# Loads of q, k and v that each wait for the fifth load ahead of them

## The chip, the cores and the metric

The kernel runs on one core of one Trainium2 chip. The metric is the device time of one execution in microseconds (us), the median over several runs. A core has five engines that run side by side, each with its own stream of instructions: TensorE (PE in the profile; its weight loads are shown apart as PEld), VectorE (DVE), ScalarE (ACT), GpSimd (POOL) and SyncE (SP). SyncE does no arithmetic here: it waits on semaphores and issues transfers (DMAs), and sixteen DMA engines move the bytes. SP issues strictly in order, so a transfer that has to wait holds up all that stands behind it on SP.

## The reference: linear attention, then a mixture of experts

For each of 8 batches and 8 heads (576 positions, 64 channels) the reference makes a 64x64 state from k and v, multiplies q by it and normalises each row. The rows of all heads, side by side, are 4608 tokens of 512 channels. A token whose skip score is positive goes to the one of 8 experts with the highest gate value, and gets that expert's output added.

```
kv  = einsum('bhsd,bhse->bhde', k, v)
o   = einsum('bhsd,bhde->bhse', q, kv)
x   = o / sqrt(mean(o*o) + 1e-6) * g_norm          # -> (4608, 512)
go  = x @ w_skip > 0
e   = argmax(x @ w_gate);  p = softmax(x @ w_gate)[e]
out = x + (go ? p * (relu(x @ w1[e]) @ w2[e]) : 0)
```

## The kernel before

**Two stages.** The first 110 us or so are attention; the rest is the experts, whose work is matrix products on PE with the experts' weights (8 x 4 MB) streamed in beside them. The change lies in the first stage.

**Loads.** For each batch b, k, v and q are each loaded as four parts (`load_part`, L116); part j holds the head pair 2j and 2j+1 for all 576 positions: 128 partitions by 9 x 64 float32, 288 KB. A batch is thus 12 loads, the whole stage 96. `load_kv` (L129) issues k part 0, v part 0, k part 1 and so on; `load_q` (L138) issues the four parts of q. All go out on SP. k and v have three buffers each, q has two, so a load of batch b+3 (or b+2 for q) also waits until PE has done with the batch that held its buffer. In program order the loads run: k and v of batch 0, q of batch 0, k and v of batch 1, q of batch 1, k and v of batch 2, then one group at a time from the loop over units (L1001 to L1005), with stores of finished rows (`store_x`, L652) between them on the same SP queue.

**Semaphores of the loads.** The framework gives each DMA of SP or ACT one of eight semaphores in turn, and a DMA waits until the one that had its semaphore before, the eighth ahead, has landed. The four small DMAs that ACT issues at the start take four of these turns. So at most eight are under way.

**Work on PE in the first stage.** `state(b, some)` (L379) is a run of small 64x64 products k^T v, accumulated in `sum_ps`; it reads parts 0 and 1 in its first half and parts 2 and 3 in its second. `state_t` and `state_m` (L406, L414) transpose the state and multiply it by the gate weights. The 36 *units* n each take half the heads (u = 0 or 1) of four of the nine 64-row chunks of one batch, or of the ninth chunks of four batches: `turn(n)` (L460) transposes q for the next unit, `values(n)` (L495) multiplies by the state; a unit with u = 0 reads q parts 0 and 1, one with u = 1 parts 2 and 3. ACT squares and copies, DVE sums, normalises and scales (`xl`, L554), POOL multiplies by g_norm (`xb`, L628). The order of all of this is written out by hand (`tc.manual_schedule()`): `at(step, part, job)` puts a job at a step of the loop over units, and each engine does its instructions in that order.

**Instructions themselves** are also brought in by DMA: the profile shows them as the kind "instruction", on queues of their own (q8 and q14).

Of the kernel before, what the change touches and what calls it, by code (L numbers as in the profile page):

```python
# [17 lines left out]
def kernel(  # L18
# [43 lines left out]
    nc = tc.nc  # L62
# [48 lines left out]
    g_ps = ps_g.tile([P, 512], FP32)  # L111
    GB = 4 * KD + 8 * G

    kts, vts, qts = {}, {}, {}

    def load_part(t, src, b, j):  # L116

        js = slice(j, j + 1)
        nc.sync.dma_start(
            out=t[:, js, :, :].rearrange("p j c d -> p j (c d)"),  # L120
            in_=src[b].rearrange("(j a) (p c) d -> (a p) j (c d)", a=2, c=C)[:, js, :])

    def load(pool, tag, src, b):
        t = pool.tile([P, 4, C, D], FP32, tag=tag, name=tag)
        for j in range(4):
            load_part(t, src, b, j)
        return t

    def load_kv(b, js=range(4)):  # L129
        if b < B:  # L130
            if js.start == 0:
                for name, to in (("k", kts), ("v", vts)):
                    to[b] = kv_pool.tile([P, 4, C, D], FP32, tag=name, name=name)
            for j in js:
                for src, t in ((k, kts[b]), (v, vts[b])):
                    load_part(t, src, b, j)
# [201 lines left out]
    def load_weights(r, pool, behind=None, later=False):  # L338
# [4 lines left out]
        if behind:  # L343
            tc.add_manual_dep(ins.ins, behind.ins.name, WAIT, reason="gathers first")
        w2 = pool.tile([P, FC, DM], FP32, tag="w2", name="w2")
# [4 lines left out]
    def load_second(r, behind=None):  # L350
# [3 lines left out]
        if behind:  # L354
            tc.add_manual_dep(ins.ins, behind.ins.name, WAIT, reason="gathers first")

# [89 lines left out]

    late = []
    todo = {}
    WAIT = mybir.DependencyInfo(mybir.DependencyClass.Sync, mybir.DependencyReason.SCHED_ONLY)

    def at(step, part, job):
        todo.setdefault((step, part), []).append(job)
# [188 lines left out]
    def scale(n, behind=None, keep=0, eng=None):  # L641

        while len(late) > keep:
            job, nq, store = late.pop(0)
            ins = job(eng or nc.gpsimd)
            if behind:
                tc.add_manual_dep(ins.ins, behind.ins.name, WAIT, reason="VectorE's port is free then")
            store = store() if store else None
# [1006 lines left out]
```

## Time and profile before

| | |
|---|---|
| median of 3 runs | 369.1 us (367.73 to 369.5) |
| the profiled execution, its own time | 368.61 us |
| its span, first to last instruction | 366.7 us |
| PE busy | 349.8 us (95%) |
| bytes moved by DMA | 81.70 MB |
| mean granted clock of TensorE | 0.997 |

The profile is of one execution. "Busy tenths in 40 slices" cuts the span into 40 pieces of 9.17 us and gives the share of each in which an engine (or, on average, the 16 DMA engines) was at work. A wait is written as the waiting engine and line, an arrow, and what ended the wait; "issue" there means that nothing that the profile shows was being waited for. "To landing" is the time from the issue of a DMA to its completion. In a timeline row stand the start, the length, the engine and line, the operation with its output and inputs, how many instructions are merged in the row, and in brackets the idle time of the engine before it.

### The profile page before, as it was taken

Reading aid. Unit: us, or ns where it says so; the run is one execution under the profiler, and the core shown is the slowest. Engines: PE = TensorE matmul, PEld = TensorE weight load, DVE = VectorE, ACT = ScalarE, POOL = GpSimd, SP = SyncE. Lnnn points to the kernel's source line nnn. Section 1 sums busy time; section 2 is a strip of 40 time slices with the busy share of each in tenths; the row PEclk is TensorE's granted clock in tenths of the full one; section 3 lists DMA queues with packets and bytes.
Section 4 is the critical chain, followed back from the end, with each engine's and each line's share of the span. In section 5 each row is a group of like instructions: output and inputs, shape, how many; then the busy total and the mean of one; then the engine's idle time right before and its main releaser. Section 6 shows DMA issues by size and latency. Waiting matters only on the chain.

```text
span 366.7 us, 9560 instructions
## 1 busy us (share of the span) xinstructions
PE 349.8 (95%) x3754; PEld 304.6 (83%) x3754; DVE 247.6 (68%) x630; ACT 147.0 (40%) x424; POOL 123.2 (34%) x201
## 2 busy tenths in 40 slices
PE   8979998999899998999999999999999999999993
PEld 4768887889779667599879988989988998989982
DVE  2646678678889553875937676686776776878821
ACT  2537675677855323345104402511431430531410
POOL 8037677757784170223032102303203203002002
PEclk9999999999999999999999999999999999999998
DMA  7999999999969479782526437365563662601001
GB/s 258 378 389 389 391 384 389 394 351 305 348 214 362 121 255 374 285 261 77 220 85 231 145 142 240 126 231 155 193 230 102 231 247 73 221 1 57 3 2 53
DMA packets 32808, 81.70 MB, mean 223 GB/s; under 512 B 3242, under 2 KB 3250, under 8 KB 32756
## 3 DMA queue, kind: packets, MB, share of 16 engines
q1 hardware_dynamic: 29264, 70.53, 54.2%
q0 software_dynamic: 3472, 10.48, 8.8%
q8 instruction: 31, 0.51, 0.5%
q14 instruction: 21, 0.17, 0.1%
q10 hardware_dynamic: 20, 0.02, 0.0%
HBM read 66.80 MB, written 14.48 MB: 222 GB/s over the span
## 4 chain that ended last, share of the span: by engine, by line
PE 79%; issue 7%; DMA 4%; DVE 3%; POOL 2%; ACT 2%; SPq 0%; POOLq 0%; DVEq 0%; ACTq 0%
PE bank L1279 45%; PE bank L1211 9%; PE o_ps L507 6%; DMA v<-in_v_dram 4%; PE sum_ps L387 4%; PE bank L1199 4%; PE q_ps L469 3%; PE bank L1180 2%; DVE xl L554 1%; DVE rs L531 1%; PE o_ps L488 1%; PE q_ps L876 1%; PE g_ps L876 1%; POOL xb L628 1%; PE g_ps L417 1%
## 5 line engine op out<-in xcount | busy, mean ns | idle before, releaser
L1289 ACT COPY p<-bank 128x128 f32<-128x128 f32 (+6 forms) x70 | 20.8, 297 | 96.8 <-PE bank L1279 89.3
L1279 PE MATMUL bank<-xt,w 128*128 128x128 f32 (+5 forms) x336 | 55.4, 288 | 0.4 <-DVE bank L1283 0.4
L1410 POOL DMA_INDIRECT out_dram<-xg,rows x14 | 14.0, 997 | 116.5 <-DVE xg L1407 114.2
L1279 PEld LDWEIGHTS bank<-xt,w 128*128 128x128 f32 x336 | 47.0, 190 | 2.3 <-DVE bank L1283 1.8
L1283 DVE TENSOR_TENSOR bank<-bank,p 128x128 f32<-128x128 f32 (+6 forms) x70 | 23.6, 337 | 30.0 <-PE bank L1279 27.6
L628 POOL TENSOR_TENSOR xb<-xl,g_b 128x512 f32<-128x512 f32 x26 | 31.7, 1221 | 15.0 <-DVE rs L545 12.1
L1279 PE MATMUL bank<-xs,s 128*128 128x128 f32 (+5 forms) x224 | 36.7, 289 | 0.0
L507 PE MATMUL o_ps<-kvd,qT 128*128 128x146 f32 x240 | 35.4, 289 | 0.7 <-DVE xl L554 0.5
L507 PEld LDWEIGHTS o_ps<-kvd,qT 128*128 128x128 f32 x240 | 31.4, 189 | 1.9 <-DVE xl L554 1.3
L1279 PEld LDWEIGHTS bank<-xs,s 128*128 128x128 f32 x224 | 31.1, 190 | 1.0 <-issue 0.5
L1211 PE MATMUL bank<-w,ht 128*32 128x128 f32 (+2 forms) x424 | 29.9, 313 | 0.0
L387 PE MATMUL sum_ps<-v,k 64*64 64x64 f32 x1152 | 24.5, 223 | 4.7 <-issue 4.3
L531 DVE TENSOR_REDUCE rs<-sq 128x8 f32<-128x512 f32 x36 | 24.5, 681 | 5.2 <-ACT sq L523 5.0
L387 PEld LDWEIGHTS sum_ps<-v,k 64*64 64x64 f32 x1152 | 20.2, 134 | 9.2 <-issue 6.1
L554 DVE TENSOR_TENSOR xl<-o_ps,rs 128x584 f32<-128x584 f32 x32 | 24.5, 766 | 3.9
L1211 PEld LDWEIGHTS bank<-w,ht 128*32 128x32 f32 (+2 forms) x424 | 18.2, 119 | 10.6 <-issue 7.2
L1279 PE MATMUL bank<-t,ht 128*128 128x256 f32 x112 | 27.0, 384 | 0.0
L1279 PE MATMUL bank<-w,ht 128*128 128x256 f32 x112 | 26.5, 380 | 0.0
L1171 POOL DMA_INDIRECT xg<-out_dram,src x14 | 13.9, 992 | 35.2 <-DMA out_dram<-xg,rows 19.0
L1279 PE MATMUL bank<-t,hs 128*128 128x256 f32 x112 | 25.3, 379 | 0.0
L523 ACT ACTIVATE sq<-o_ps 128x512 f32<-128x512 f32 x34 | 20.2, 595 | 11.3 <-PE o_ps L507 10.5
L1279 PEld LDWEIGHTS bank<-t,ht 128*128 128x128 f32 x112 | 20.8, 190 | 3.9 <-issue 1.2
(217 smaller groups left out, 671.9 us busy)
## 6 DMA issues: line engine op xcount, KB each, us to landing
w<-in_moe_w_dram SPq DMA_DIRECT2D x16, 2048.0 KB, 10.1
k<-in_k_dram SPq DMA_DIRECT2D x32, 288.0 KB, 6.0
v<-in_v_dram SPq DMA_DIRECT2D x32, 288.0 KB, 6.2
q<-in_q_dram SPq DMA_DIRECT2D x32, 288.0 KB, 6.0
out_dram<-xb SPq DMA_DIRECT2D x25, 256.0 KB, 5.9
out_dram<-w SPq DMA_DIRECT2D x8, 256.0 KB, 5.5
out_dram<-xb POOLq DMA_DIRECT2D x3, 256.0 KB
xg<-out_dram,src POOLq DMA_INDIRECT x16
```

Source lines behind the costliest of these rows:

```text
L387: nc.tensor.matmul(out=sum_ps[w * 64:(w + 1) * 64, a, u, :], lhsT=kt[r, 2 * u + w, c, :], rhs=vt[r, 2 * u + w, c, :], start=(c == 0), stop ...
L507: mm = nc.tensor.matmul(out=ps[:, w, 0:2 * PK].rearrange("p (r k) -> p r k", r=2)[:, :, cols], lhsT=qT[:, w, a, :], rhs=kvds[b % KVD][:, w ...
L523: nc.scalar.activation(out=sq[:, :, :, :], in_=heads(ps, G, G + 2 * D), func=ACT.Square)
L531: nc.vector.tensor_reduce(out=rs[:, :, :], in_=sq[:, :, :, :].rearrange("p x y (a d) -> p x (y a) d", a=2), axis=AX.X, op=ALU.add)
L554: nc.vector.tensor_tensor(out=xl[:, :, :, :].rearrange("p x y (a k) -> p x (y a) k", a=2), in0=ps[:, :, 0:2 * PK].rearrange("p x (h k) -> ...
L628: late.append((lambda eng: eng.tensor_tensor(out=xb[:, :, 4 * u * D:(4 * u + 4) * D].rearrange("p r (w x) -> p r w x", w=2), in0=xl[:, :, ...
L1199: nc.tensor.matmul(out=hps[:, cols], lhsT=w_sb[r][0][:, dc, f * P:(f + 1) * P], rhs=xt[:, dc, cols], start=(dc == 0), stop=(dc == DC - 1))
L1211: nc.tensor.matmul(out=yps[q * m:(q + 1) * m, 0:n], lhsT=ht(f)[:, off:off + m], rhs=w_sb[r][1][:, f, q * n:(q + 1) * n], start=(f == 0), s ...
L1279: nc.tensor.matmul(out=out, lhsT=lhsT(i), rhs=rhs(i), start=start and i == 0, stop=i == k - 1, skip_group_check=True)
L1283: nc.vector.tensor_tensor(out=to, in0=x, in1=y, op=ALU.add)
L1289: nc.scalar.copy(out=t, in_=x)
L1410: ins = nc.gpsimd.indirect_dma_start(out=cut_rows(m)[:, :], out_offset=bass.IndirectOffsetOnAxis(ap=rows[:, col:col + 1], axis=0), in_=x, ...
```

## The change

Each load of q, k or v, from the thirteenth in program order on, gets one more dependency: on the load five places ahead of it in the list of these loads. Stores are not in that list. The first twelve loads (k, v and q of batch 0) are left as they were. The line that makes `WAIT` only moves up. Nothing else changes: no other engine's instructions, no sizes, no order.

```diff
-    kts, vts, qts = {}, {}, {}
+    kts, vts, qts, loads = {}, {}, {}, []
+    PACED, DEPTH = 12, 5
+    WAIT = mybir.DependencyInfo(mybir.DependencyClass.Sync, mybir.DependencyReason.SCHED_ONLY)
 
     def load_part(t, src, b, j):
 
         js = slice(j, j + 1)
-        nc.sync.dma_start(
+        ins = nc.sync.dma_start(
             out=t[:, js, :, :].rearrange("p j c d -> p j (c d)"),
             in_=src[b].rearrange("(j a) (p c) d -> (a p) j (c d)", a=2, c=C)[:, js, :])
+        if len(loads) >= PACED:
+            tc.add_manual_dep(ins.ins, loads[-DEPTH].ins.name, WAIT, reason="a short queue")
+        loads.append(ins)
...
-    WAIT = mybir.DependencyInfo(mybir.DependencyClass.Sync, mybir.DependencyReason.SCHED_ONLY)
```

What SP waits for, on SP's stream from the twelfth load on. In these rows `DMAHW0` to `DMAHW7` are the eight semaphores of SP's and ACT's DMAs, and the loads take them in turn (the first load of the kernel has `DMAHW4`). Before:

```order
L119 DMA q_110<-in_q_dram 128x576 [waits DMAHW7_49]
L119 DMA k_269<-in_k_dram 128x576 [waits DMAHW0_49]
L119 DMA v_270<-in_v_dram 128x576 [waits DMAHW1_49]
L119 DMA k_269<-in_k_dram 128x576 [waits DMAHW2_49]
L119 DMA v_270<-in_v_dram 128x576 [waits DMAHW3_49]
L119 DMA k_269<-in_k_dram 128x576 [waits DMAHW4_49]
L119 DMA v_270<-in_v_dram 128x576 [waits DMAHW5_49]
```

and with the change:

```order
L121 DMA q_110<-in_q_dram 128x576 [waits DMAHW7_49]
L121 DMA k_269<-in_k_dram 128x576 [waits DMAHW3_49,DMAHW0_49]
L121 DMA v_270<-in_v_dram 128x576 [waits DMAHW4_49,DMAHW1_49]
L121 DMA k_269<-in_k_dram 128x576 [waits DMAHW5_49,DMAHW2_49]
L121 DMA v_270<-in_v_dram 128x576 [waits DMAHW6_49]
L121 DMA k_269<-in_k_dram 128x576 [waits DMAHW7_49]
L121 DMA v_270<-in_v_dram 128x576 [waits DMAHW0_49]
```

The thirteenth load (the first of k of batch 1) waited for the eighth DMA ahead of it, and now waits for the fifth load ahead too; from the sixteenth on the nearer wait stands alone, since it implies the farther one.

Later on SP, around the load of q of batch 3 (`q_759`), where two stores stand between the loads. Before:

```order
L119 DMA k_595<-in_k_dram 128x576 [waits DMAHW2_49]
L119 DMA v_596<-in_v_dram 128x576 [waits DMAHW3_49]
L670 DMA out_0_dram<-xb_485 64x1024 [waits DMAHW4_49,Pool_49]
L670 DMA out_0_dram<-xb_485 64x1024 [waits DMAHW5_49]
L119 DMA q_759<-in_q_dram 128x576 [waits DMAHW6_49,PE_49]
L119 DMA q_759<-in_q_dram 128x576 [waits DMAHW7_49]
L119 DMA q_759<-in_q_dram 128x576 [waits DMAHW0_49]
L119 DMA q_759<-in_q_dram 128x576 [waits DMAHW1_49]
```

and with the change:

```order
L121 DMA k_595<-in_k_dram 128x576 [waits DMAHW5_49]
L121 DMA v_596<-in_v_dram 128x576 [waits DMAHW6_49]
L674 DMA out_0_dram<-xb_485 64x1024 [waits Pool_49]
L674 DMA out_0_dram<-xb_485 64x1024
L121 DMA q_759<-in_q_dram 128x576 [waits DMAHW7_49,PE_49]
L121 DMA q_759<-in_q_dram 128x576 [waits DMAHW0_49]
L121 DMA q_759<-in_q_dram 128x576 [waits DMAHW1_49]
L121 DMA q_759<-in_q_dram 128x576 [waits DMAHW2_49]
```

The k and v loads wait three places nearer; the stores wait for POOL alone (what they waited for before has already been waited for by the load ahead of them); and the q loads wait only one place nearer than before, since the two stores between are not counted.

## The prediction, made before the changed kernel was run

> **What bounds the kernel now.** First the head of the page, then the slices of DMA use.
>
> ```profile
> span 366.7 us, 9560 instructions
> PE 349.8 (95%) x3754; PEld 304.6 (83%) x3754; DVE 247.6 (68%) x630; ACT 147.0 (40%) x424; POOL 123.2 (34%) x201
> DMA  7999999999969479782526437365563662601001
> GB/s 258 378 389 389 391 384 389 394 351 305 348 214 362 121 255 374 285 261 77 220 85 231 145 142 240 126 231 155 193 230 102 231 247 73 221 1 57 3 2 53
> q8 instruction: 31, 0.51, 0.5%
> k<-in_k_dram SPq DMA_DIRECT2D x32, 288.0 KB, 6.0
> ```
>
> PE is the engine that is nearly always at work, and the end of the kernel is PE's. But in the first eight slices (to 73 us) the DMA engines are full as well, at 378 to 394 GB/s. A load of 288 KB (294,912 bytes) at 392 GB/s takes 0.75 us, and 6.0 us from issue to landing is eight times that: the loads stand in a line of eight and come out one each 0.75 us. So in that stretch a load lands when the line has moved on, not when it was issued.
>
> Next, who waits: PE and POOL in the first 110 us, SP to 75 us.
>
> ```profile
> PE sum_ps L387 <- issue: 4.3, 3, 2.4
> PE sum_ps L387 <- DMA v<-in_v_dram: 0.3, 1, 0.3
> ...
> POOL xb L628 <- DVE rs L545: 12.1, 17, 2.1
> ...
> SPq L119 <- DMA k<-in_k_dram: 9.2, 22, 0.9
> SPq L119 <- PE g_ps L409: 1.1, 1, 1.1
> ```
>
> PE waits for a load once, for 0.3 us. Its longest idle is three stalls, 4.3 us in all, in the middle of `state`, and nothing the profile names ends them. SP waits mostly for loads and little for PE's buffers, so the loads set their own pace. PE's timeline has the stalls, and one more row that matters:
>
> ```profile
> 24.47 0.62 PE L387 MATMUL sum_ps<-v,k 64*64 64x64 f32 x25 [2.43 <-issue]
> 45.69 0.66 PE L469 MATMUL q_ps<-ident,q 128*128 128x128 f32 x4
> 63.38 0.57 PE L387 MATMUL sum_ps<-v,k 64*64 64x64 f32 x21 [0.99 <-issue]
> 69.87 0.56 PE L387 MATMUL sum_ps<-v,k 64*64 64x64 f32 x19 [0.84 <-issue]
> ```
>
> What are the stalls? From one to the next I count instructions, and ask which instruction transfers run in the 1.2 us before each ends (the windows 22.0 to 23.2, 60.7 to 61.9, 67.3 to 68.5):
>
> ```profile
> 24.40:63.30 38.90, 37.17 (x755) 32.77 (x755) 27.43 (x61) 27.07 (x73) 27.85 (x55) 1.00 1.05 388
> 63.30:69.80 6.50, 5.64 (x126) 5.08 (x127) 5.29 (x13) 3.27 (x8) 5.13 (x8) 1.00 1.05 392
> ...
> q8 instruction: 1, 0.02, 5.6%
> ...
> q8 instruction: 1, 0.02, 5.7%
> ...
> q8 instruction: 1, 0.02, 5.6%
> ```
>
> The first two counts are PE's products and weight loads: 1510 and 253 instructions, that is six times 252 and once 253. The q8 queue brings 31 blocks of 16 KB for 7508 such instructions, 242 each. Each window holds one block, and the stall ends 1.3 to 1.5 us after its window closes. So PE has come to the end of a block and the next one has not arrived: the stalls are late instruction fetches. One thing is missing: no row shows when a fetch is asked for. If it is asked for when PE begins the block before (251 instructions earlier, about 57.6 us for the second stall and 63.4 for the third), the block starts to move 3.1 and 3.9 us after that.
>
> **The change, part by part.** *Loads under way: 8 to 5.* Nothing is removed, and no instruction is added on PE, DVE, ACT or POOL. On SP a load is issued three landings later, 3 x 0.75 = 2.25 us. Does it land later? With five under way the line gives each load 5 x 0.75 = 3.75 us from issue to landing. A load that meets no line needs this long (the k loads issued in the first 2 us, and, as the far bound, the rate at 4.9 to 11.5 us, when five to eight loads were under way):
>
> ```profile
> DMA to landing us min/median/max: 3.5/4.0/4.5
> ...
> 4.90:11.50 6.60, 6.46 (x138) 3.91 (x140) 2.59 (x28) 0.72 (x3) 3.29 (x6) 1.00 0.98 335
> 12.00:45.60 33.60, 30.80 (x607) 27.21 (x601) 19.08 (x43) 21.34 (x57) 17.13 (x33) 1.00 1.05 392
> ```
>
> 3.5 is under 3.75, by 0.25 us only: the line still just closes, and loads land when they landed before. Bounds of what this costs: nothing, or the rate falls from 392 to 335 GB/s. At that rate the 42 loads from the thirteenth to the fifty-fourth take 0.88 instead of 0.75 us each, 5.4 us more. I take 1% of the 33.6 us, 0.3 us, an estimate near the lower bound, because the full-rate row covers five times the stretch and the early row also has loads at its start that wait for ACT's small ones.
>
> *Does a later load hold PE up?* The row of PE at 45.69 is the first turn of q of batch 3, which reads parts 0 and 1. Part 3 was issued and landed so:
>
> ```profile
> 41.93 0.43 SPq L119 DMA_DIRECT2D q<-in_q_dram  x1
> ...
> DMA to landing us min/median/max: 5.2/5.2/5.2
> ```
>
> 41.93 + 5.2 = 47.1, and two landings earlier part 1 came, at 45.6. PE used it at 45.69: a margin under 0.1 us. So up to here PE cannot run ahead of the loads, whatever stalls it is spared; and every us by which loads fall behind by then is lost to PE at once. Hence the 2.43 us stall at 22.05 is worth nothing if it goes: PE would only wait at 45.6 for q instead. That is the next thing late.
>
> *The two later stalls.* After 45.69 the loads are further ahead. The tighter ones are those of q, with two buffers where k and v have three. For batch 4: issue of the parts, their time to landing, and the first turn on PE; for the last part of batch 7, issue and landing, and the turn that reads it:
>
> ```profile
> 51.89 2.12 SPq L119 DMA_DIRECT2D q<-in_q_dram  x4
> DMA to landing us min/median/max: 6.3/6.3/6.3
> 60.88 0.63 PE L469 MATMUL q_ps<-ident,q 128*128 128x128 f32 x4
> ...
> 87.93 0.43 SPq L119 DMA_DIRECT2D q<-in_q_dram  x1
> DMA to landing us min/median/max: 5.4/5.4/5.4
> 96.78 0.66 PE L469 MATMUL q_ps<-ident,q 128*128 128x128 f32 x4
> ```
>
> The four parts of batch 4 are all issued by 54.0 and landed by 60.3; part 3 of batch 7 lands at 93.3 and is used at 96.78. Here a stall that goes is PE's gain. If a fetch block stands in the same line as the loads, its wait shrinks with the line: three loads fewer are 2.25 us less. The stalls need only 0.99 and 0.84 us (1.13 and 0.98 on the weight loads), so both go even if the block feels half of that. Is the gain on the chain? The chain from 58 to 75 us:
>
> ```profile
> 62.39 0.99 issue
> 63.38 0.57 PE sum_ps L387 x21
> ...
> 68.34 1.18 POOL xb L628
> 69.52 1.36 issue
> ```
>
> The second stall is on it. At 69.52 the chain moves to POOL; POOL's own row there,
>
> ```profile
> 70.90 0.85 POOL L400 COPY kvd<-both 64x256 f32<-64x256 f32 x2 [1.39 <-ACT both L394]
> ```
>
> waits for the copy of the state, which waits for the products that the third stall holds up. So both count: 0.99 + 0.84 = 1.8 us. All engines after that follow PE, and the margin of 3.5 us at q of batch 7 is more than what they gain, so 1.8 us passes to the end.
>
> *Queued behind the waiting loads on SP* are the stores L670. They go out about 2 us later, but still into a full DMA line. Who waits for them is POOL, for an `xb` buffer; POOL's waits before L628 are for DVE in the row above (12.1 us, 17 times), so the six buffers cover it: nothing, and up to 2.25 us a store if that cover were gone. The double waits of a few loads cost SP an instruction or so beside an issue of 0.33 us each 0.75 us: nothing.
>
> *The sum.* -1.8 us (two stalls) + 0 (first stall, absorbed at q of batch 3) + 0.3 (rate) = -1.5 us. The profiled execution took 368.61 us, so 367.1; it stood 0.5 us under the median of 369.1, so I put the median at **367.6 us**.
>
> **The rivals.** *The fetch does not stand in the loads' line.* If each DMA engine takes packets in turn from its queues, a fetch waits for one packet of 2 KB, not for the loads ahead, and a shorter line changes nothing: the stalls stay, and with 0.3 us for the rate the time is 369.4 us. For it: block delays after the assumed request differ much while the line is always full. Against it: in the full stretch the block moves 3 to 4 us after the request, far more than one packet of about 0.1 us. The Trainium skill, "DMA: Bandwidth & Descriptors", section "Queues, rings and completion order", says just this of the engines: they go round between the queue rows, one packet from each. By that rule the two stalls keep their 1.8 us; the 3.1 and 3.9 us above speak against it, though they rest on an assumed time of request.
>
> *The line no longer closes, slower.* The price is at q of batch 3, 45.6 us, the first place without margin. If a load needs more than 3.75 us from semaphore to landing, each load after the twelfth comes later by a fifth of the excess, 42 times. At 4.1 us this is 0.07 x 42 = 2.9 us; less 1.8 for the stalls, +1.1; from 4.2 us on it is slower by over 0.5%. At the early rate (5.4 us) it would be +3.6, 372.7 us. For it: only 0.25 us of margin, and the 16 engines do not finish a load together, so a short line starves the quick ones. Against: landings are regular to a few hundredths of a us at 392 GB/s.
>
> *Fetches everywhere gain.* ACT, DVE and POOL fetch instructions too, and PE's idle of 0.5 to 0.8 us on DVE and ACT at 58, 95 and 99 us might shrink a little: -1.8 and another 1 us, 366.3 us. Little speaks for it; those waits have named causes.
>
> **How the numbers follow.** Forecast (both stalls go, the rate about holds): 0.42. Fetch unchanged: 0.20. Slower rate: 0.24. More gained: 0.14. No change is what this kernel's measurement cannot tell from 369.1, within 0.5% or 1.85 us. The forecast at -1.5 lies close to that edge: I count a third of it, 0.14, as faster. Faster 0.14 + 0.14 = 0.28; slower 0.24; same 0.48. Range: from 366.0 (more gained, with the spread of the three runs) to 371.2 (a rate loss of some 4 us less the stalls); outside are the larger rate losses and a rest below, about 0.2. The forecast's own range is 366.6 to 368.4.
>
> **What would show it.** Right: k, v and q land a median of 3.7 to 4 us after issue; the slices to 73 us keep 385 GB/s or more; the rows of PE at 62 and 69 us have no idle; q of batch 3 is turned at 45.6 to 46 us, with a wait for q before it if the first stall went. Wrong: landing still 5 to 6 us; slices at 370 or less, and PE waiting for q, k or v by more than 1 us; stalls of the old size with the shorter line. What would break the sum is chiefly the margin of 0.25 us.

## The result and the profile after

The changed kernel takes **379.1 us** (median of 6 runs, 375.69 to 380.97) against 369.05 us beside it (6 runs, 367.73 to 370.72): a ratio of **1.025**, 95% interval 1.0215 to 1.029. It is slower by 10 us. The prediction, 367.6 us with a range to 371.2, was wrong, and in sign. Medians and ratios leave out runs over 1.5% above the fastest of their kernel: four of the ten with six loads under way (376.2 us and more), three of the ten with seven (372.1 us and more), the profiled ones among them, and two of the nineteen beside those.

The profiled execution took 378.42 us. The head, the slices, two shares of the chain and two DMA groups of its page:

```profile
span 376.5 us, 9562 instructions
PE 354.7 (94%) x3754; PEld 308.1 (82%) x3754; DVE 248.5 (66%) x630; ACT 146.9 (39%) x424; POOL 123.8 (33%) x201
PEclk9999899998799999999999999999999999999998
DMA  7989999999999849955626363672762662700001
GB/s 270 338 296 364 328 323 315 337 314 326 346 329 282 298 124 339 390 196 214 205 80 216 118 225 85 221 265 60 248 223 81 246 219 95 251 1 34 24 1 53
PE 67%; DMA 22%; issue 6%; DVE 3%; POOL 1%; SPq 0%; ACT 0%; POOLq 0%; DVEq 0%
k<-in_k_dram SPq DMA_DIRECT2D x32, 288.0 KB, 5.0
q<-in_q_dram SPq DMA_DIRECT2D x32, 288.0 KB, 5.3
```

From 9 to 75 us the DMA tenths still read 9, but for one slice of 8, while the rate has gone from 378 to 394 GB/s down to 296 to 364: the engines count as busy and move less. A load lands 5.0 to 5.3 us after its issue (median), where I had expected 3.7 to 4. The chain that ended last has 22% of DMA in place of 4%. The chain before was

```profile
PE 79%; issue 7%; DMA 4%; DVE 3%; POOL 2%; ACT 2%; SPq 0%; POOLq 0%; DVEq 0%; ACTq 0%
```

In the PEclk row of the changed kernel three slices (38 to 47, 85 to 94 and 94 to 104 us) have fallen to 8, 8 and 7 tenths.

The changed kernel by windows, with the columns as in the prediction (the last three are granted clock, DMA share and GB/s):

```profile
12.00:45.60 33.60, 27.80 (x496) 24.53 (x495) 15.90 (x37) 17.44 (x48) 13.97 (x27) 0.95 0.96 324
39.90:43.40 3.50, 3.50 (x45) 3.31 (x44) 1.66 (x3) 1.88 (x8) 1.40 (x2) 0.51 0.97 321
91.20:98.00 6.80, 5.91 (x52) 5.06 (x53) 2.42 (x7) 1.95 (x4) 1.39 (x2) 0.50 0.99 371
```

In the stretch that ran at 392 GB/s before, the rate of all transfers is now 324: 294,912 bytes each 0.91 us instead of 0.75. Twice TensorE runs at half clock, for 3.4 and 6.8 us. Who waits on PE up to 112 us:

```profile
PE q_ps L473 <- DMA q<-in_q_dram: 7.1, 7, 2.3
PE sum_ps L392 <- issue: 1.6, 2, 1.0
PE sum_ps L392 <- DMA v<-in_v_dram: 1.4, 2, 0.7
```

Waits for loads were 0.3 us and are now 8.5 us; the stalls by late instructions were 4.3 us and are 1.6. Where this happens, in PE's timeline:

```profile
23.04 0.62 PE L392 MATMUL sum_ps<-v,k 64*64 64x64 f32 x25 [1.03 <-issue]
...
37.64 0.41 PE L473 MATMUL q_ps<-ident,q 128*128 128x128 f32 x2 [2.26 <-DMA q<-in_q_dram]
38.92 0.44 PE L473 MATMUL q_ps<-ident,q 128*128 128x128 f32 x2 [0.87 <-DMA q<-in_q_dram]
...
50.52 0.66 PE L473 MATMUL q_ps<-ident,q 128*128 128x128 f32 x4
...
68.51 0.57 PE L392 MATMUL sum_ps<-v,k 64*64 64x64 f32 x21 [0.57 <-issue]
...
91.48 0.66 PE L473 MATMUL q_ps<-ident,q 128*128 128x128 f32 x2 [1.74 <-DMA q<-in_q_dram]
...
110.54 0.38 PE L957 MATMUL g_ps<-rows,again 128*128 128x1 f32 x2 [0.82 <-DVE rows L953]
```

The last of these rows stands near the end of the attention stage; before it was

```profile
100.50 0.38 PE L953 MATMUL g_ps<-rows,again 128*128 128x1 f32 x2 [0.81 <-DVE rows L949]
```

So the first turn of q of batch 3 is 4.8 us late (50.52 for 45.69), and the last row 10.0 us (110.54 for 100.50). The span is 9.8 us longer. In this execution all of the loss is in the attention stage; the experts neither add nor give back.

SP's timeline shows how the loads have become slow. Before, around 20 us:

```profile
18.78 0.33 SPq L119 DMA_DIRECT2D k<-in_k_dram  x1
19.53 0.33 SPq L119 DMA_DIRECT2D v<-in_v_dram  x1
20.29 0.33 SPq L119 DMA_DIRECT2D k<-in_k_dram  x1
21.05 0.33 SPq L119 DMA_DIRECT2D v<-in_v_dram  x1
```

and with the change:

```profile
13.45 0.33 SPq L121 DMA_DIRECT2D k<-in_k_dram  x1
15.78 0.33 SPq L121 DMA_DIRECT2D v<-in_v_dram  x1
16.52 0.33 SPq L121 DMA_DIRECT2D k<-in_k_dram  x1
...
20.99 1.13 SPq L121 DMA_DIRECT2D k<-in_k_dram  x1
23.37 0.33 SPq L121 DMA_DIRECT2D v<-in_v_dram  x1
```

An issue mostly tells of a landing here, since SP waits for one: 70 of the 84 loads from the thirteenth on are issued within 0.1 us of the landing of the fifth load ahead. Before, one comes each 0.75 us. After, most still do (eight in a row from 15.78 to 20.99 us), but now and then there is a gap of 1.2 to 2.4 us (13.45 to 15.78, 20.99 to 23.37). From 10.5 to 80 us I count 15 gaps of over 1.1 us between the issues on SP, stores included, 13.3 us more than 0.75 us each; before there are 7 with 4.2 us. So between the gaps the line of five does close, and the rate of 0.91 us a load is an average over even stretches and gaps. Not every gap is a late landing: that before 26.36 us follows an issue that itself took SP 1.46 us, and that before 45.29 us a store whose issue took 1.60 us.

### The profile page after: what moved, and what is told of

Its sections match the earlier page's. It is cut to its first block, busy times and chain, and to the rows that moved or that the text cites. A ratio compares the mean times of both kernels' runs of the same rounds, so it can differ in the third digit from the quotient of the medians.

```text
span 376.5 us, 9562 instructions
## 1 busy us (share of the span) xinstructions
PE 354.7 (94%) x3754; PEld 308.1 (82%) x3754; DVE 248.5 (66%) x630; ACT 146.9 (39%) x424; POOL 123.8 (33%) x201
## 4 chain that ended last, share of the span: by engine, by line
PE 67%; DMA 22%; issue 6%; DVE 3%; POOL 1%; SPq 0%; ACT 0%; POOLq 0%; DVEq 0%
PE bank L1283 44%; PE bank L1215 9%; DMA k<-in_k_dram 7%; DMA q<-in_q_dram 7%; DMA v<-in_v_dram 7%; PE bank L1203 4%; PE o_ps L511 2%; PE bank L1184 2%; PE q_ps L473 2%; PE sum_ps L392 1%; DVE xl L558 1%; DVE rs L535 1%; PE q_ps L880 1%; PE g_ps L783 1%; PE g_ps L880 1%
## 5 line engine op out<-in xcount | busy, mean ns | idle before, releaser
L511 PE MATMUL o_ps<-kvd,qT 128*128 128x146 f32 x240 | 36.9, 297 | 0.6 <-DVE xl L558 0.5
L511 PEld LDWEIGHTS o_ps<-kvd,qT 128*128 128x128 f32 x240 | 32.9, 196 | 1.6 <-DVE xl L558 1.1
L473 PE MATMUL q_ps<-ident,q 128*128 128x128 f32 x128 | 23.2, 298 | 7.3 <-DMA q<-in_q_dram 7.1
L476 ACT COPY qT<-q_ps 128x512 f32<-128x512 f32 x32 | 18.8, 586 | 19.8 <-PE q_ps L473 19.3
```

The costliest lines, as they stand in the source:

```text
L473: nc.tensor.transpose(out=ps[:, w, :, hf, :], in_=qts[b][:, 2 * u + w, c:c + 2, :], identity=ident[:, :])
L476: nc.scalar.copy(out=qT[:, :, :, :].rearrange("p w a t -> p (w a t)"), in_=ps[:, :, :, :, :].rearrange("p w a h t -> p (w a h t)"))
L511: mm = nc.tensor.matmul(out=ps[:, w, 0:2 * PK].rearrange("p (r k) -> p r k", r=2)[:, :, cols], lhsT=qT[:, w, a, :], rhs=kvds[b % KVD][:, w ...
```

## The experiments

Two theories were set against each other. Both start from what the profile after shows, that five loads under way do not keep the rate of eight.

- **HOLES.** A load lands with the slowest of its sixteen shares, one on each DMA engine. When one engine is held for a while by other packets (a 16 KB block of instructions, for one), the line of five has no spare load to keep the other fifteen busy, and a hole is left; a line of eight has 2.25 us of spare.
- **LONG LOOP.** With other loads under way each load simply needs some 4.6 us from issue to landing, evenly, and the rate is the number under way divided by that.

A third question came up from the windows above: how much of the 10 us is the half clock.

### How many under way: d6 and d7

```diff
-    PACED, DEPTH = 12, 5
+    PACED, DEPTH = 12, 6      # d6; d7 has 7
```

> The changed kernel with a line of six loads in place of five. Two theories. HOLES: a load lands with the slowest of its sixteen shares, and a 16 KB instruction block or a burst of POOL stores holds one share for about 1 us; a line of five has 5 x 0.75 = 3.75 us against some 3.5 us for a load by itself, so each hold becomes a hole in the landings (SP's timeline of the changed kernel: 0.75 us from issue to issue, with holes of 2.0 to 2.4 us); with six there is 0.75 us more to cover each hold, so holes shrink to 1.3 to 1.6 us, and q of batch 3 lands about 1.5 to 2.5 us later than before: 369.5 to 372 us. LONG LOOP: each load needs about 4.6 us from semaphore to landing once others are under way (5 loads of 294,912 bytes at 325 GB/s); six give 0.77 us a load, evenly spaced, q of batch 3 lands 0.7 us late: 367 to 369.5 us.

> The changed kernel with a line of seven. Both theories: the rate is that of before (385 GB/s or more to 73 us), q of batch 3 is turned at 45.5 to 46.5 us; the median within 0.5% of before. If a shorter line also speeds up PE's instruction fetches, the stalls at 62 and 69 us shrink by up to half, 0.9 us in all.

Measured: with six 372.2 us (374.6 over all ten), with seven 368.5 us, against 369.2 us beside them. The ratios are **1.0065** (1.0014 to 1.0115) and **0.996** (0.992 to 0.9997). The same window as above, six loads under way:

```profile
12.00:45.60 33.60, 30.07 (x549) 26.73 (x547) 17.17 (x40) 19.73 (x54) 15.34 (x31) 0.95 1.00 352
```

and seven:

```profile
12.00:45.60 33.60, 30.77 (x571) 27.59 (x562) 17.81 (x39) 20.38 (x55) 16.59 (x32) 0.95 1.02 371
```

Five, six, seven and eight loads under way give 324, 352, 371 and 392 GB/s, in one execution each. As an average over the stretch, no number stands out from which the line closes. Worked out as time for the whole line (number x 294,912 bytes / rate): 4.55, 5.03, 5.56 and 6.02 us, about 0.5 us for each load more. So the first five are dear: within these bounds a load from issue to landing takes, on average, about 2.1 us and 0.49 us for each load in the line, an estimate from these four rates, and not 3.5 us or the line's 0.75 us each, whichever is longer. The marks of the landings agree roughly: the median from issue to landing of the loads that land in this window is 4.7, 5.1, 5.8 and 6.2 us. The four rates do not fix the order of six and seven: from 45.6 to 73 us the same profiles have 324, 352, 345 and 388 GB/s, and there seven under way in another kernel (late7, below) have 379.

On the theories: with six, q of batch 3 was first turned at 48.09 us, 2.4 us later than before, which LONG LOOP had put at 0.7 us and HOLES at 1.5 to 2.5; SP's gaps were uneven, 1.2 to 1.85 us.

```profile
48.09 0.97 PE L473 MATMUL q_ps<-ident,q 128*128 128x128 f32 x4
```

So HOLES had the arrival of q right and LONG LOOP did not. The kernel's time of 372.2 us is just above the range of HOLES (369.5 to 372) and well above that of LONG LOOP (367 to 369.5). With seven, the time was as both had it; the rate was not (371 GB/s for 385 or more), nor was the first turn of q of batch 3 (47.05 us for 45.5 to 46.5).

### One half of the stage: early and late

```diff
-        if len(loads) >= PACED:
+        if PACED <= len(loads) < 52:       # early: only the 13th to the 52nd load
```

```diff
-    PACED, DEPTH = 12, 5
+    PACED, DEPTH = 52, 5                   # late: only from the 53rd load on
```

> Only the loads from the thirteenth to the fifty-second wait for the fifth ahead (up to the end of q of batch 3), later ones do not. If the loss is in the arrival of q of batches 2 and 3, where PE had under 0.5 us of margin, most of the 10 us is here: PE waits for q of batches 2 and 3 as in the changed kernel, turns q of batch 3 at about 50.5 us, and later loads (rate back at 388 GB/s) are not waited for: 374 to 376 us. If the loss is mainly in the later waits for q of batches 5 and 6 and in the second stretch of half clock at 91 us, it is 371 us or less.

> Only the loads after the fifty-second wait for the fifth ahead. To 46 us all is as before. Then loads come at 0.9 us instead of 0.75: q of batch 4 some 2.5 us late against 2.5 us of margin, q of batch 5 about 4.5 against 5.5, q of batch 6 6 to 7 against 4.6: a wait of about 2 us for q of batch 6, and, if that idle time halves the clock as at 91 us in the changed kernel, some 1.7 to 3.4 us more; less up to 1.8 us for the fetch stalls: 369 to 373 us. If the margins hold and the stalls go: 367.5 us, under before.

Measured: early 375.67 us (372.19 to 377.36), ratio **1.017** (1.011 to 1.023); late 373.62 us (371.3 to 375.53), ratio **1.012** (1.0055 to 1.018). Against 369.2 us that is +6.4 and +4.4 us, each give or take some 2 us by its interval, and the sum is about the change's 10. The early kernel is as expected for a loss that lies mainly there, the late one 0.6 us over its range. Both halves lose; where the prediction had a margin (3.5 us at q of batch 7) it is used up as well. The late kernel's PE at q of batch 6:

```profile
86.63 0.44 PE L473 MATMUL q_ps<-ident,q 128*128 128x128 f32 x2 [1.77 <-DMA q<-in_q_dram]
```

and the early kernel's at q of batch 2, the first place where it waits for q:

```profile
36.23 0.41 PE L473 MATMUL q_ps<-ident,q 128*128 128x128 f32 x2 [1.39 <-DMA q<-in_q_dram]
38.05 0.44 PE L473 MATMUL q_ps<-ident,q 128*128 128x128 f32 x2 [1.42 <-DMA q<-in_q_dram]
```

### Late, with seven: late7

```diff
-    PACED, DEPTH = 12, 5
+    PACED, DEPTH = 52, 7
```

> Only the loads after the fifty-second wait, and for the seventh ahead in place of the fifth. Both theories: arrival as before up to q of batch 3; after it a line of seven keeps the rate; PE's fetch stalls at 62 and 69 us (0.99 and 0.84 us) shrink or go, as they did with a line of seven throughout: 367.5 to 369 us, 0 to 0.5% under before.

Measured: 366.3 us (364.77 to 368.96, 12 runs) against 367.39 us, ratio 0.997 (0.994 to 1.0004). It cannot be told from the kernel before. The stalls were expected to shrink or go, and one by late instructions stands in its profile at 62 us, longer than the 0.99 us of before:

```profile
65.06 0.91 PE L392 MATMUL sum_ps<-v,k 64*64 64x64 f32 x21 [2.57 <-issue]
```

So a line of seven is no sure cure for these stalls.

### Holding one DMA engine: one5, one8, all5, all8, big5, big8

To test HOLES by itself, transfers into a buffer that nobody reads are added on GpSimd's queue, extra work in each of these six kernels. A row of 4099 floats goes as one packet through one DMA engine; a row of 4096 is spread over all.

```diff
+    extra = nc.dram_tensor("extra", (6, 4099), FP32, kind="Internal").ap()   # all5, all8: 4096
...
+    for i, step in enumerate(range(2, 14, 2)):
+        at(step, "end", lambda i=i: nc.gpsimd.dma_start(
+            out=extra[i:i + 1, :], in_=moe_w1[0:1].rearrange("e d f -> e (d f)")[:, 0:4099]))
```

one5 and all5 add this to the changed kernel, one8 and all8 to the kernel before.

> The changed kernel with six more transfers on GpSimd's queue, at units 2, 4, 6, 8, 10 and 12 (about 20 to 52 us): each copies 16,396 bytes from DRAM to DRAM as one row of a prime length (4099 float32), so that it should run on one of the sixteen DMA engines, as an instruction block does. HOLES: each such transfer holds one share of the loads in line by 0.5 to 1 us, so it makes further holes in the landings; q of batch 3 lands 2 to 4 us later than in the twin of 4096 elements, and the time is 2 to 5 us over the twin's. LONG LOOP: 0.1 MB more is 0.25 us; no difference from the twin.

> The twin: the same six transfers with 4096 elements each, a length that can be spread over sixteen DMA engines. Both theories: about the changed kernel's own 379 us, plus at most 1 us for GpSimd's time to issue them.

> The kernel before with the six one-engine transfers. HOLES: a line of eight has some 2.5 us to cover a share that is held, so q of batch 3 lands under 1 us later than in the twin and the time is within 1 us of the twin's. LONG LOOP: no difference from the twin.

> The kernel before with the six transfers of 4096 elements. Both theories: the kernel before's own time, plus at most 1 us for GpSimd's time to issue them.

Measured: one5 379.79, all5 377.93, one8 367.91, all8 369.54 us, against 369.74 us before; ratios 1.028 (1.020 to 1.036), 1.025 (1.015 to 1.0345), 0.998 (0.994 to 1.001) and 1.0005 (0.997 to 1.004). A packet of one engine held it for 0.6 to 0.7 us. Part 1 of q of batch 3 landed at 51.97 in one5 and 51.94 in all5, at 45.15 in one8 and 45.06 in all8: no difference, where HOLES had 2 to 4 us with five under way. The hold may have been too short. So a longer one:

```diff
+    extra = nc.dram_tensor("extra", (4, 12289), FP32, kind="Internal").ap()
...
+    for i, step in enumerate(range(2, 10, 2)):       # big5: on the change; big8: on the kernel before
```

> The changed kernel with four larger one-engine transfers on GpSimd's queue, at units 2, 4, 6 and 8 (about 28 to 45 us), 49,156 bytes each as one row of 12289 float32. The ones of 16,396 bytes held an engine 0.6 us (one packet of 612 to 739 ns), little over the 0.25 us that a line of five leaves; these should hold it 1.8 to 2 us. HOLES: each makes a hole of about 1.6 us in the landings, so q of batch 3 lands 4 to 6.5 us later than the 51.6 us of the changed kernel, 55.5 us or later, and the time is 383 to 388 us. LONG LOOP: 0.2 MB more is 0.5 us: q of batch 3 at 52.5 us at most, 378 to 381 us.

> The kernel before with the same four transfers of 49,156 bytes. HOLES: a line of eight has some 2.5 us to cover a share that is held, more than the 1.8 to 2 us: q of batch 3 lands within 1 us of 45.6 us, 368.5 to 371 us. If a held share costs a line of eight as much as a line of five: q of batch 3 at 50 us or later, 374 us or more. LONG LOOP: 0.5 us, as with five.

Measured: big5 379.8 us, ratio 1.033 (1.027 to 1.038); big8 371.96 us, ratio **1.010** (1.005 to 1.0155), against 367.39 us. The packets held one engine for 1.8 to 2.7 us each. PE at q of batch 3 in big8 and, below, in big5:

```profile
50.02 0.41 PE L470 MATMUL q_ps<-ident,q 128*128 128x128 f32 x2 [4.32 <-DMA q<-in_q_dram]
```

```profile
53.11 0.41 PE L474 MATMUL q_ps<-ident,q 128*128 128x128 f32 x2 [3.56 <-DMA q<-in_q_dram]
```

Holding one engine of sixteen for four times 1.8 us, 7.3 us of 16 x 30 us of engine time, makes q of batch 3 4.3 us late with eight under way. That it is the one engine shows in the completion marks (each of the sixteen shares of a load gives one): of part 0 of q of batch 3 in big8 fifteen shares were in by 44.97 us, and the last came at 49.89, just ahead of PE's turn at 50.02. A rival is that POOL, busy with the added issues, held up the stores and with them the loads behind them on SP; but from 30 to 52 us SP waited for POOL once, for 0.4 us. No twin of these four with the same bytes over all engines was run; at 392 GB/s their 197 KB would be 0.5 us. So the first half of HOLES holds: a load lands with its slowest share. The other half does not hold for a hold of this length: eight loads are not immune, and the line of five lost less by it, not more. Its first turn of q of batch 3 came at 53.11, 1.2 to 2.7 us later than in the other profiles with five under way throughout (50.39 to 51.87), and its time of 379.8 us is within 1.1 us of the changed kernel's, where HOLES had 383 to 388. LONG LOOP, which had 0.5 us for both, had the time of big5 right and the delay of q wrong in both.

What the marks add on the line itself: before, a load's shares come in over 2.4 us (the median from 12 to 73 us; 1.2 to 3.8), for one load from 26.38 to 28.79 us, for the next from 27.13 to 29.52. In the changed kernel the median is 1.9 us (0.7 to 2.7); they come within 0.8 us in one even stretch (28.23 to 29.07), and with one straggler at some gaps (fifteen by 14.98, the last at 16.50). In the line of eight the engines drift 2.4 us apart, which is about all that three more loads can cover (3 x 0.75 us); its cover is in use already, so a further long hold is paid. In the line of five the quick ones would run dry and wait. This fits these runs, but that drift is the *cause* of the lower rate was argued from the marks and not tried by itself. The Trainium skill, "DMA: Bandwidth & Descriptors", section "Why a DMA increments its semaphore by 16 and not by 1", says that the engines of one transfer finish independently and that the semaphore counts them; the marks agree.

What holds an engine in the changed kernel, where nothing is added? The trace has the kernel's own instruction blocks, 16 KB in one packet that takes 0.9 to 1.6 us. Of the ten that start between 10 and 80 us, eight (at 13.02, 20.82, 32.61, 50.84, 57.97, 66.22, 70.59 and 75.91 us) are followed by one of SP's gaps that ends 2.5 to 2.8 us after the block's start (15.78, 23.37, 35.31, 53.59, 60.58, 68.89, 73.36 and 78.62 us); these eight make up 7.4 of the 13.3 us. In the second profile of the changed kernel it is seven of ten, before the change one of eleven. So HOLES, with instruction blocks of 1 us as the hold, is the better account of a good half of the gaps. The added packets agree: in big5 each of the four is followed by a gap that ends 2.8 to 3.1 us after its start, in one5 three of the six (2.2 to 2.5 us), in one8 none. But all this is agreement in time, and no run here takes the instruction blocks away.

### How much is the half clock: fill, after2, fill6

Each half-clock stretch stands at waits for q: the first, from 39.96 us, 1 us behind the waits that end at 37.64 and 38.92, the second, from 91.16 us, begins within the wait that ends at 91.48. `dense(8)`, eight products on tiles long landed whose result nobody reads, keeps PE at work there; it is extra work of 1.9 us each.

```diff
         ...
+            if n + 1 in (starts[2], starts[6]):                    # fill
+            if n + 1 in (starts[2], starts[6], starts[6] + 1):     # fill6
+                dense(8, ps_q.tile([P, 512], FP32, tag="q", name="q_ps"))
```

> The changed kernel with eight dummy products on PE (128x128 by 128x512 in bf16, 0.26 us each, 2.1 us) ahead of the first turn of q of batch 2 and of batch 6, where PE waited 2.3 and 1.7 us for q. They use no result. CLOCK: in the changed kernel's trace the granted clock is half for 3.4 us from 40 us and for 6.8 us from 91 us, right after these waits, which costs 1.7 + 3.4 us; if idle time of PE does this, the products keep the clock up, q is there when they end, and the time is 374 to 376.5 us with a granted clock of 0.99 or more. If the clock drops for another reason: 378 to 381 us.

Measured: 376.97 us (375.6 to 377.32), ratio 1.024 (1.019 to 1.0295); the clock rose from 0.984 to 0.993, and the time did not come down to the 374 to 376.5 us expected. Since it had a half-clock stretch left at 93.66 us, the third wait was filled as well, beside the changed kernel itself.

> The changed kernel again, beside the one with filled waits. Both theories: 1.020 to 1.030 of the kernel before; profiled with a stretch of TensorE at half clock right behind the wait for q of batch 3 or of batch 6.

> The changed kernel with eight dummy products on tiles long landed ahead of the first turn of the queries of batch 3, and ahead of the first and the second turn of batch 7 (batches 2, 6 and 6 counted from nought). CLOCK ADDS (the half clock behind the wait for q of batch 6 lies on the path, 3.4 us): 3 us or more below the changed kernel of the same call. LOADS BOUND (the row of the last attention batch is set by the arrival of q, k and v, and work lost to the clock is caught up in waits that shrink): within 1.5 us of it, waits for q still in the profile, and the reciprocal at the end of the attention stage no more than 1 us earlier.

Measured: the changed kernel again 378.71 us, ratio 1.028 (1.023 to 1.033); filled 379.0 us, ratio 1.030 (1.025 to 1.034). The clock of the filled one's profiled execution is 0.998, no slice is below 9 tenths, and its row at the end of the stage comes no sooner:

```profile
94.95 1.90 PE L177 MATMUL q_ps<-ones 128*128 128x512 bf16 x8
96.91 0.66 PE L473 MATMUL q_ps<-ident,q 128*128 128x128 f32 x4
...
110.30 0.38 PE L957 MATMUL g_ps<-rows,again 128*128 128x1 f32 x2 [0.81 <-DVE rows L953]
```

110.30 against 110.54. By what was put down, LOADS BOUND holds and CLOCK ADDS fell. I do not read it as clean as that. Part 3 of q of batch 6 landed at 95.9 us in this execution, so of the 1.9 us of products that end at 96.85 some 0.9 us was paid. And the runs of one kernel tell something else: of the twelve runs of the changed kernel those with a clock of 0.991 to 0.995 have spans of 373.9 and 374.4 us, those with 0.978 to 0.981 have 377.0 to 379.2, some 3 us for each 0.01. A run that waits more may also lose its clock by that, so the slope is a bound. The mean clock is 0.985 in the twelve and 0.994 in the runs of before beside the last six, so **at most some 3 of the 10 us go through the clock**. At an equal clock (0.995) the spans are 373.9 against 365.1 to 366.1 us, and at 0.991 to 0.992 they are 374.4 against 367.3 to 369.0: 5 to 9 us are left, by these few runs, for the loads.

The second profile of the changed kernel shows that the place of the loss shifts. Its windows and PE rows:

```profile
38.00:41.00 3.00, 2.61 (x11) 2.62 (x12) 0.94 (x2) 1.05 (x3) 0.79 (x1) 0.50 1.02 380
90.00:95.00 5.00, 4.75 (x98) 4.09 (x97) 2.77 (x9) 2.80 (x7) 1.75 (x3) 1.00 1.02 388
```

```profile
102.87 0.44 PE L473 MATMUL q_ps<-ident,q 128*128 128x128 f32 x2 [2.55 <-DMA q<-in_q_dram]
...
107.70 0.38 PE L957 MATMUL g_ps<-rows,again 128*128 128x1 f32 x2 [0.45 <-DVE rows L953]
...
114.93 0.63 PE L869 MATMUL q_ps<-ident,xg 128*128 128x128 f32 x4 [1.86 <-DMA xg<-out_dram,src]
...
117.79 0.41 PE L869 MATMUL q_ps<-ident,xg 128*128 128x128 f32 x2 [1.57 <-DMA xg<-out_dram,src]
```

Here PE waits 1.3 and 0.3 us for q of batch 6 (up to 89.89 and 90.55 us) and the clock is whole behind it, the row at the end of the stage comes 2.8 us sooner than in the first profile, and 3.4 us are then lost waiting for the first gathered tokens; its span is 376.9 us, the other's 376.5.

## Why the prediction was wrong

**The line "just closes": wrong as an average, and this is the step that failed.** The term "I take 1% of the 33.6 us, 0.3 us" of the sum measured, by the prediction's own way, 0.91 - 0.75 = 0.16 us a load, 6.4 us over the 40 loads from the thirteenth to the fifty-second. (The 42 rows that the prediction counted from SP's list hold two stores.) Part 3 of q of batch 3, which was reckoned as 41.93 + 5.2 = 47.1 us, now comes 6.3 us after an issue at 47.2, at 53.5 us: 6.4 us later (5.0 in the second profile), where the prediction's upper bound was 5.4. The upper bound was the right end. I compared 3.75 us with the 3.5 us of a load that meets no line and called the difference a margin; the row that gave the 3.5 had it as the least of 3.5/4.0/4.5, and its median was over 3.75 already. The comparison itself is at fault too: with six the line would have been 4.5 us long and the margin 1 us, and it still lost 40 GB/s. In the even stretches five under way do come each 0.75 us. What the term put at nothing is the load that comes late: a gap of up to 1.6 us over the 0.75, with no spare load in the line to make it up. The row at 335 GB/s, which came from a stretch where five to eight loads were under way, was near the rate that came, and I set it aside; that it was so near has some luck in it, for the same window, 4.9 to 11.5 us, has 367 GB/s in the changed kernel.

**q of batch 3 as the first place without margin: nearly.** q of batch 2 came first, with waits of 2.26 and 0.87 us in the first profile; the prediction had not looked at its margin, about 0.4 us. From there every late load is lost to PE, as said.

**The first stall is worth nothing: right.** It shrank from 2.43 to 1.03 us (0.41 in the second profile), and the kernel had nothing of it.

**The two later stalls go: right in direction, and worthless.** At 62 us there is none, at 69 us 0.57 us is left (0.84 before), and the early and late kernels have at most 0.72 us there. They were shorter by some 1.3 us, but PE waits for loads in that stretch, so nothing comes through. The rival by which a fetch does not stand in the loads' line had these stalls stay, which with five under way they did not. That the shorter line took them away is not shown: with seven one grew to 2.57 us, and one8, with eight under way, has neither of them.

**Margin from batch 4 on (3.5 us at q of batch 7): it was there and was used up**, since the loads go on losing: the eighty-fourth lands at 84.0 us for 73.5, 10.5 us later, where the fifty-second was 6.4 us later. The late kernel, whose first 52 loads are as before, loses its 4.4 us by this; its profile has waits of 0.6 and 1.8 us for q of batch 6 and one of 2.1 us for gathered tokens.

**The rival "the line no longer closes, slower" was right in mechanism and nearly in place**, and its price of 372.7 us was 6.4 us too low: it stopped counting at q of batch 3. What it left out is the second half of the stage (4.4 us by the late kernel), the half clock behind PE's waits, at most 3 us; and it took off 1.8 us of stalls that brought nothing. The three overlap, for they add up to more than 6.4 us.

## What to carry to other kernels

A transfer alone says how long it takes when it has every engine to itself; how many must be under way to fill the line has to be read from a stretch in which that many *are* under way, and the average rate fell with the number (here 392, 371, 352, 324 GB/s for eight to five, one execution each), without an edge on which a margin could be reckoned. A line that just closes has no spare transfer for one that comes late, so ask what can hold an engine, the kernel's own instruction blocks included. Where the transfers pace the work, a shorter line costs at every load, so count all of them to the end of the stage and not to the first place that has no slack. Busy tenths of the DMA engines hardly show it (9 in both kernels, but for one slice of 8); the GB/s row does.

## What the runs showed of the hardware

- Three loads fewer under way cost 17% of the rate (392 to 324 GB/s) although the DMA engines read 9 tenths busy, but for one slice of 8 (0.96 for 1.05 from 12 to 45.6 us).
- One DMA engine of sixteen, held four times for 1.8 us, made q of batch 3 4.3 us late with eight loads of 288 KB under way, its last share 4.9 us behind the fifteenth; held for 0.6 to 0.7 us six times it had no effect that could be seen.
- Of ten instruction blocks of 16 KB (0.9 to 1.6 us each) eight were followed by a gap in the loads that ended 2.5 to 2.8 us after the block's start with five loads under way, and one of eleven with eight.
- Waits of 2.3 and 0.9 us on PE close together were followed by 3.41 us at half clock; a stretch of 6.83 us began within a wait of 1.7 us. The Trainium skill, "TensorE: Matmul & The Clock Gate", section "What's actually happening", has the gate decide by windows of 3413 ns that run freely; both lengths are whole windows of that. At the second place the second profile (90 to 95 us) has no such stretch, behind waits of 1.3 and 0.3 us; whether the shorter waits or where the windows lie made the difference, no run here shows.
